# Attention bias from its 32 hidden units: relu tiles in float32 and one float32 product per tile, in place of on/off masks and two rounds of split bf16 products

## The chip, the cores and the metric

One core of a Trainium2 chip runs the whole program. The metric is the device time of one execution in microseconds (us); the kernel before takes 932.72 us (median of three runs, 932.68 to 932.83). The core's engines work side by side: PE (TensorE, matrix products; PEld is its weight load), DVE (VectorE), ACT (ScalarE), POOL (GpSimd), and SP (SyncE), which here only starts DMA transfers. Each engine runs its own instructions in the order in which they are written; semaphores make it wait for others.

## The reference, cut to what matters

Attention with a learned position bias is followed by two dense blocks, which the change leaves alone. The bias is computed once and used by all four batches:

```python
pos = np.arange(S)                                    # S = 576
psi_rel = np.log1p(np.abs(rel))                       # rel = i - j
psi_i = np.log1p(np.maximum(pos[:, None], 1.0))
x = (psi_rel / psi_i)[..., None]
h = np.maximum(x @ w1 + b1, 0.0)                      # 32 hidden units
bias = h @ w2                                         # 8 heads
scores = scores + bias.transpose(2, 0, 1)[None]
```

For one row i, x depends on |i - j| alone. So a row of the bias is a table over the distance 0, 1, 2, ..., laid out once forwards and once mirrored. Everything is float32 at the interface.

## The kernel before, in words

The program has four stages one after another: the bias (class `Bias`), attention, a gated block and a last block. Only the first stage and what hands it over are touched.

`Bias` works in 36 groups of 16 rows i; `order` takes groups 32 to 35 first and then 0 to 31. Group g needs `width(g)` distances: 304 to 576, summed over the 36 groups 15840, so 440 on average. A group has 4 tiles. A tile has 128 partitions, which are 4 rows times 32 hidden units, and along it lie the distances; `self.lt` holds log1p of the distance in every partition. The weights of the second layer are set up so that the product of a tile gives 32 partitions (4 rows times 8 heads), which go to one quarter of the columns of PE's array (`tile_position=(0, 32 * q)`). The four tiles of a group so fill one PSUM tile `ps` of 128 partitions (16 rows times 8 heads).

Before, `masks` (L163) does not compute relu. It writes a bf16 tile `mk` that says where a unit is on (1 or 0): ACT does 7 of 16 tiles with a steep sigmoid (L169), DVE the others with a comparison (L171). What the unit then adds is a line in x, a slope and a constant, both linear in the mask. `products(n, 0)` multiplies the masks by the slopes, DVE multiplies the result in PSUM by x (L207), and `products(n, 1)` adds the constants, one group later, into the same PSUM tile. The weights `cb` are float32 numbers split into three bf16 parts, so each of the two rounds takes 3 products per tile, or 6 where the width is over 512 (`parts` is 2). All products are on L189.

Then ACT copies `ps` to `rs` (L214), POOL writes the mirrored half beside it (`pool_round`, L54; for the last group DVE, L218), SP writes `rs` to DRAM (`write`, on L47, 295.5 KB), and `beside(n)` puts one step of the first attention pair behind it on POOL's or SP's queue: loads of q, k, v, their split into high and low parts on POOL, moves of these by DMA, and `load_bias`, which reads finished rows of the bias back from DRAM. The numbers 24, 27 and 30 in `beside` say behind which group.

`AHEAD = 2`: the tiles of a group are made two groups before their products. There are 17 buffers for `mk`, 6 for `rs` and 4 PSUM tiles, which are all of PSUM. When the stage ends its pools are closed, and attention's take the same memory: the first scores wait for PSUM from the last copies, and the last two bias tiles are read back once the last write has landed.

Of the kernel before, what the change touches and what calls it, by code (L numbers as in the profile page):

```python
# [17 lines left out]
S = 576  # L18
# [65 lines left out]
class Bias:  # L84
# [9 lines left out]
    ROW = 2 * S  # L94
    MID = S - 1
    AHEAD = 2
    ON_ACT = 7

    def __init__(self, ch, i, dram):
        self.ch, self.nc, self.i = ch, ch.nc, i  # L100
# [24 lines left out]
    def open(self):  # L125
        ch, nc, i = self.ch, self.nc, self.i
        cp = ch.pool(self.ctx, "bc", "right")
        self.wp = ch.pool(self.ctx, "bw", "right")
        self.pp = ch.pool(self.ctx, "bp", "right", bufs=4, space=PSUM)
        con = cp.tile([128, 194], F, name="con")  # L130
        self.lt = cp.tile([128, S], F, name="lt")
        nc.sync.dma_start(con, i["small"])
        nc.scalar.dma_start(self.lt, i["ltab"])
        sm, ip4, self.ip16 = con[:, :14], con[:, 14:158], con[:, 158:194]
        self.nb = cp.tile([128, 2], F, name="nb")
        self.scl = cp.tile([128, 144], F, name="scl")
        self.scb = cp.tile([128, 144], F, name="scb")
        cab = cp.tile([128, 16], F, name="cab")
        cf = cp.tile([128, 2, 32], F, name="cf")
        self.cb = cp.tile([128, 3, 2, 32], B, name="cb")  # L140

        self.warm = cp.tile([128, 2], F, name="warm")
        nc.gpsimd.memset(self.warm, 0.0)
        nc.scalar.activation(self.warm, self.warm, AF.Sigmoid)
        ts = nc.vector.tensor_scalar
        big = float(2.0**60)
        ts(out=self.nb[:, 1:2], in0=sm[:, 1:2], scalar1=big, scalar2=None, op0=ALU.mult)
        ts(out=self.scb, in0=ip4, scalar1=sm[:, 0:1], scalar2=big, op0=ALU.mult, op1=ALU.mult)
        ts(out=self.nb[:, 0:1], in0=sm[:, 1:2], scalar1=-1.0, scalar2=None, op0=ALU.mult)
        ts(out=self.scl, in0=ip4, scalar1=sm[:, 0:1], scalar2=None, op0=ALU.mult)  # L150
        for ab in range(2):
            ts(out=cab[:, 8 * ab : 8 * ab + 8], in0=sm[:, 2:10], scalar1=sm[:, ab : ab + 1], scalar2=8.0, op0=ALU.mult, op1=ALU.mult)

            nc.vector.tensor_tensor(
                out=cf[:, ab].rearrange("p (r h) -> p r h", r=4), in0=sm[:, 10:14].unsqueeze(2).to_broadcast([128, 4, 8]),
                in1=cab[:, 8 * ab : 8 * ab + 8].unsqueeze(1).to_broadcast([128, 4, 8]), op=ALU.mult,
            )
        for n in range(3):
            nc.vector.tensor_copy(self.cb[:, n], cf)
            if n < 2:  # L160
                nc.vector.tensor_tensor(out=cf, in0=cf, in1=self.cb[:, n], op=ALU.subtract)

    def masks(self, g):  # L163
        out = []
        w = self.width(g)
        for t in range(4 * g, 4 * g + 4):
            m = self.wp.tile([128, S], B, tag="mk", name="mk", bufs=4 * self.AHEAD + 9)
            if (self.no * self.ON_ACT) % 16 < self.ON_ACT:
                self.nc.scalar.activation(m[:, :w], self.lt[:, :w], AF.Sigmoid, bias=self.nb[:, 1:2], scale=self.scb[:, t : t + 1])  # L169
            else:  # L170
                self.nc.vector.tensor_scalar(  # L171
                    out=m[:, :w], in0=self.lt[:, :w], scalar1=self.scl[:, t : t + 1], scalar2=self.nb[:, 0:1], op0=ALU.mult, op1=ALU.is_gt
                )
            self.no += 1
            out.append(m)
        return out

    def run(self, beside):
        nc = self.nc
        order = list(range(32, 36)) + list(range(32))  # L180
        mq = [self.masks(g) for g in order[: self.AHEAD]]
        G = {}

        def products(n, ab):
            ps, mk, parts, ln = G[n]
            for at in range(parts):
                for part in range(3):
                    for q in range(4):
                        nc.tensor.matmul(  # L189
                            ps[32 * q : 32 * q + 32, at, :ln], self.cb[:, part, ab], mk[q][:, at * ln : at * ln + ln],  # L190
                            start=ab == part == 0, stop=part == 2, tile_position=(0, 32 * q), skip_group_check=ab > 0,
                        )

        for n in range(len(order) + 1):
            if n < len(order):
                g = order[n]
                w = self.width(g)
                parts = 1 if w <= 512 else 2
                ps = self.pp.tile([128, 2, 512], F, tag="ps", name="ps")
                ln = w // parts  # L200
                G[n] = (ps, mq.pop(0), parts, ln)
                products(n, 0)
                if n + self.AHEAD < len(order):
                    mq.append(self.masks(order[n + self.AHEAD]))
                a = ps[:, :parts, :ln]
                lt = self.lt[:, :w].rearrange("p (a b) -> p a b", a=parts)
                nc.vector.scalar_tensor_tensor(out=a, in0=lt, scalar=self.ip16[:, g : g + 1], in1=a, op0=ALU.mult, op1=ALU.mult)  # L207
            if n:
                g = order[n - 1]
                w, r = self.width(g), 16 * g + 15  # L210
                products(n - 1, 1)
                ps, _, parts, ln = G.pop(n - 1)
                rs = self.wp.tile([128, 2 * S], F, tag="rs", name="rs", bufs=6)
                nc.scalar.copy(rs[:, r : r + w].rearrange("p (a b) -> p a b", a=parts), ps[:, :parts, :ln])  # L214
                if n < len(order):
                    self.ch.pool_round(rs[:, :r], rs[:, r + 1 : 2 * r + 1][:, ::-1])
                else:
                    nc.vector.tensor_copy(rs[:, :r], ps[:, 0, 1 : r + 1][:, ::-1])  # L218
                self.write(g, rs)
                beside(n - 1)  # L220
        nc.scalar.activation(self.warm, self.warm, AF.Exp)


class Attention:
# [320 lines left out]
class Gated:  # L545
# [11 lines left out]
    def __init__(self, ch, i, x_d, x2_d, gw_d, g_d):  # L557
# [669 lines left out]
def tile_kernel(tc, i, out):  # L1227
    with tc.manual_schedule(), tc.tile_pool(name="dram", bufs=1, space=DRAM) as dp:
        x_d = [dp.tile([2, DM, S], F, name="x_d%d" % b) for b in range(NB)]
        x2_d = [dp.tile([DM, TC], F, name="x2_d%d" % c) for c in range(NC)]  # L1230
        gw_d = dp.tile([FF, DM], F, name="gw_d")
        g_d = [dp.tile([FF, TC], F, name="g_d%d" % c) for c in range(NC)]
        ch = Chip(tc)

        ga = Gated(ch, i, x_d, x2_d, gw_d, g_d)
        ga.open_keep()
        bias = Bias(ch, i, dp)
        bias.open()
        at = Attention(ch, i, bias, x_d, ga)
        at.open_left()  # L1240

        def beside(n):

            at.start(n)
            if n == 7:
                at.load_bias(0, 0)
            if n in (1, 2):
                at.load_ab(n - 1)
            if n == 24:
                at.load_bias(0, 1, 2)  # L1250
            if n == 27:
                at.load_bias(0, 5, 6)
            if n == 30:
# [96 lines left out]
```

## Time and profile before

| | us |
|---|---|
| median of the runs | 932.72 |
| the profiled execution | 937.69 |
| its span | 935.9 |
| first and last on/off tile begun on DVE | 6.2 and 64.2 |
| last write of the stage issued | 70.0 |
| DVE busy between 6 and 70 | 61.5 of 64 |

The span runs from the first to the last instruction of the profiled execution; 1.8 us lie around it, and the profiled execution is 5.0 us longer than the median of the runs. A view by stretches gives each engine's busy time in a stretch; a timeline gives start, length and form of instructions, with neighbours of one kind merged (x7). A length there can run past the start of the next instruction on the same engine, so the cost of one is read from start to start.

### The profile page before, as it was taken

What the parts mean: (1) busy time and instruction counts of PE and PEld (TensorE: products, weight loads), DVE (VectorE), ACT (ScalarE), POOL (GpSimd) and SP (SyncE); (2) the same over time, 40 slices, a digit from 0 to 9 for tenths busy, and PEclk for the clock granted to TensorE, in tenths of its full rate; (3) what the DMA queues carried; (4) which work ended last, traced back from release to release, by engine and by line L of the source; (5) the groups of instructions that cost most, each with busy time, mean ns of one, the idle gap of its engine ahead of it and who ended that gap; (6) DMA issues with size and microseconds to landing.
All of it is one profiled execution on the core that took longest, in us unless ns stands there. A gap on an engine that the chain in (4) does not pass through costs nothing.

```text
span 935.9 us, 16914 instructions
## 1 busy us (share of the span) xinstructions
PE 862.0 (92%) x5836; PEld 780.1 (83%) x5836; DVE 665.2 (71%) x1497; ACT 509.6 (54%) x1081; POOL 394.7 (42%) x460
## 2 busy tenths in 40 slices
PE   5877999999989988988999998999999999999998
PEld 4446998998989977987889888999999788888886
DVE  8989998998979988887764286752445765555442
ACT  7986998998878954434332133241333644444432
POOL 3337888887868643020110003742234442222200
PEclk9998999999999999998999999999999999999999
DMA  4997999898898667674351385673323211111001
GB/s 135 302 308 201 219 275 248 228 270 233 205 272 219 159 208 231 204 240 155 133 166 34 124 271 173 229 225 99 112 87 111 82 34 55 48 46 46 23 23 46
DMA packets 98389, 151.60 MB, mean 162 GB/s; under 512 B 16384, under 2 KB 62848, under 8 KB 98304
## 3 DMA queue, kind: packets, MB, share of 16 engines
q1 hardware_dynamic: 91248, 140.80, 51.3%
q10 hardware_dynamic: 7056, 9.74, 2.9%
q8 instruction: 46, 0.75, 0.3%
q14 instruction: 39, 0.32, 0.1%
HBM read 81.40 MB, written 41.30 MB: 131 GB/s over the span
## 4 chain that ended last, share of the span: by engine, by line
PE 59%; DVE 19%; DMA 12%; issue 5%; ACT 3%; SPq 2%; POOL 1%; ACTq 0%; DVEq 0%; POOLq 0%
PE ab L79 5%; PE ab L80 5%; PE ab L81 5%; DMA k<-kr 4%; PE op L463 4%; PE tp L420 4%; PE o L80 4%; PE o L79 4%; PE o L81 4%; PE sp L379 4%; DVE mk L171 3%; PE x L80 3%; PE x L81 3%; PE x L79 3%; DVE etl L511 2%
## 5 line engine op out<-in xcount | busy, mean ns | idle before, releaser
L79 PE MATMUL ab<-xh,ab 128*128 128x384 f32 x320 | 109.8, 343 | 7.7 <-DVE a L795 5.4
L410 POOL TENSOR_SCALAR e<-e,st 128x576 f32<-128x576 f32 x128 | 95.0, 752 | 33.9 <-DVE st L406 28.2
L80 PE MATMUL ab<-xl,ab 128*128 128x384 f32 x320 | 108.7, 340 | 0.0
L81 PE MATMUL ab<-xh,ab 128*128 128x384 f32 x320 | 108.7, 340 | 0.0
L511 DVE TENSOR_TENSOR etl<-tp,eth 128x512 fp32r<-128x512 f32 (+1 forms) x160 | 99.3, 629 | 8.8 <-ACT eth L497 6.7
L379 PE MATMUL sp<-k,q 128*128 128x288 f32 x512 | 91.0, 302 | 15.2 <-DVE st L392 6.4
L399 ACT ACTIVATE e<-e,st 128x576 f32<-128x576 f32 x128 | 100.1, 782 | 5.7 <-DVE st L392 5.5
L392 DVE CUSTOM_DVE_ANT_0 e<-sp,bt 128x576 f32<-128x576 f32 x128 | 95.6, 748 | 8.5 <-PE sp L379 8.3
L497 ACT CAST eth<-tp 128x512 fp32r<-128x512 f32 (+1 forms) x160 | 85.2, 543 | 28.7 <-PE tp L420 22.2
L747 POOL TENSOR_TENSOR xs<-xh,xl 128x384 f32<-128x384 f32 x20 | 24.2, 1224 | 173.6 <-DMA xl<-x_d 47.6
L420 PE MATMUL tp<-idt,e 128*128 128x128 f32 x576 | 88.7, 277 | 8.5 <-DVE etl L511 4.5
L379 PEld LDWEIGHTS sp<-k,q 128*128 128x128 f32 x512 | 76.3, 192 | 17.8 <-issue 7.8
L420 PEld LDWEIGHTS tp<-idt,e 128*128 128x128 f32 x576 | 70.0, 142 | 13.5 <-issue 6.0
L80 PE MATMUL x<-gl,wf 128*128 128x384 f32 x192 | 65.9, 343 | 8.5 <-DVE gl L62 8.5
L79 PEld LDWEIGHTS ab<-xh,ab 128*128 128x128 f32 x320 | 60.9, 190 | 11.2 <-DVE a L795 7.8
L189 PE MATMUL ps<-mk,cb 128*32 128x264 bf16 (+17 forms) x1056 | 48.8, 323 | 19.8 <-DVE ps L207 12.5
L463 PE MATMUL op<-eth,v 128*128 128x288 f32 x256 | 66.3, 340 | 0.4 <-ACT o L499 0.4
L1175 POOL TENSOR_TENSOR st<-st,half 128x1 f32<-128x1 f32 x18 | 9.9, 552 | 131.9 <-DVE st L1174 131.9
L79 PE MATMUL x<-gh,wf 128*128 128x384 f32 x192 | 65.1, 339 | 0.0
L81 PE MATMUL x<-gh,wf 128*128 128x384 f32 x192 | 65.1, 339 | 0.0
L189 PEld LDWEIGHTS <-cb 128*32 128x32 bf16 x1056 | 31.2, 98 | 37.0 <-issue 24.0
L80 PEld LDWEIGHTS ab<-xl,ab 128*128 128x128 f32 x320 | 61.0, 190 | 0.4 <-DVE xl L756 0.4
(209 smaller groups left out, 2355.7 us busy)
## 6 DMA issues: line engine op xcount, KB each, us to landing
bias_d<-rs SPq DMA_DIRECT2D x36, 295.5 KB, 4.5
qkr<-in_qk SPq DMA_DIRECT2D x16, 608.0 KB, 5.4
k<-kr SPq DMA_DIRECT2D x32, 288.0 KB, 6.5
x_d<-o SPq DMA_DIRECT2D x64, 144.0 KB, 3.9
g_d<-a ACTq DMA_DIRECT2D x48, 192.0 KB, 2.9
gl<-g_d SPq DMA_DIRECT2D x48, 192.0 KB, 2.8
k<-kr SPq DMA_DIRECT2D x32, 256.0 KB, 6.4
raw<-in_wo SPq DMA_DIRECT2D x16, 512.0 KB, 5.6
```

The source lines that it names most:

```text
L79: mm(out, a[0], b[0], start=first, stop=False, skip_group_check=more)
L80: mm(out, a[0], b[1], start=False, stop=False, skip_group_check=more)
L81: mm(out, a[1], b[0], start=False, stop=last, skip_group_check=more)
L189: nc.tensor.matmul(ps[32 * q : 32 * q + 32, at, :ln], self.cb[:, part, ab], mk[q][:, at * ln : at * ln + ln], start=ab == part == 0, stop= ...
L379: nc.tensor.matmul(ps[:, half, :HS], w["q"][:, h, q * 128 : q * 128 + 128], w["k"][:, h, x, half * HS : half * HS + HS], start=x == 0, sto ...
L392: self.nc.vector.tensor_tensor_reduce(out=halves(e), in0=ps[:, :, :HS], in1=halves(self.BT[(self.pairs[n][0], k)]), scale=-0.125, scalar=3e38,
L399: self.nc.scalar.activation(e, e, AF.Exp, bias=st[:, c : c + 1], scale=-1.0, accum_out=st[:, 2 + c : 3 + c])
L410: self.nc.gpsimd.tensor_scalar(out=e, in0=e, scalar1=st[:, c : c + 1], scalar2=1.0, op0=ALU.mult, op1=ALU.mult)
L420: tr = lambda c, src: nc.tensor.transpose(ps[: src.shape[1], c * 128 : c * 128 + 128], src, self.idt)
L463: nc.tensor.matmul(w["op"][:, half, :HS], lhs, rhs, start=c == 0 and x == 0, stop=c == 4 and x == 1)
L497: self.nc.scalar.copy(hi, src)
L511: self.nc.vector.tensor_tensor(out=lo, in0=src, in1=hi.bitcast(F), op=ALU.subtract)
```

## The change: what it does, and the diff

`masks` now makes relu itself, in float32, in a whole group at a time: groups with n % 8 in (2, 6), 9 of 36, on ACT (Relu), the other 27 on DVE, which takes the larger of scale times distance and minus b1, that is relu less a constant. One float32 product per tile (two where the width is over 512) takes the place of the 6 or 12 bf16 ones. DVE's work in PSUM (L207) is gone. ACT's copy adds the constant that DVE's groups lack: `cst`, which PE makes once at the start from the biases. There are 14 buffers for `mk`, each of twice the bytes; the read-backs in `beside` come one group earlier, the last group is mirrored on POOL, and the table of ACT's functions that is loaded at the start is already the one that attention uses.

```diff
-            m = self.wp.tile([128, S], B, tag="mk", name="mk", bufs=4 * self.AHEAD + 9)
-            if (self.no * self.ON_ACT) % 16 < self.ON_ACT:
-                self.nc.scalar.activation(m[:, :w], self.lt[:, :w], AF.Sigmoid, bias=self.nb[:, 1:2], scale=self.scb[:, t : t + 1])
+            m = self.wp.tile([128, S], F, tag="mk", name="mk", bufs=4 * self.AHEAD + 6)
+            if self.on_act(n):
+                self.nc.scalar.activation(m[:, :w], self.lt[:, :w], AF.Relu, bias=self.nb[:, 1:2], scale=self.scl[:, t : t + 1])
             else:
                 self.nc.vector.tensor_scalar(
-                    out=m[:, :w], in0=self.lt[:, :w], scalar1=self.scl[:, t : t + 1], scalar2=self.nb[:, 0:1], op0=ALU.mult, op1=ALU.is_gt
+                    out=m[:, :w], in0=self.lt[:, :w], scalar1=self.scl[:, t : t + 1], scalar2=self.nb[:, 0:1], op0=ALU.mult, op1=ALU.max
                 )
...
+    def on_act(self, n):
+        return n % 8 in (2, 6)
...
+        ps = self.pp.tile([128, 2, 512], F, tag="ps", name="ps")
+        for q in range(4):
+            nc.tensor.matmul(ps[32 * q : 32 * q + 32, 0, :2], self.cf, self.nb, start=True, stop=True, tile_position=(0, 32 * q))
+        nc.vector.tensor_copy(self.cst[:, 0:1], ps[:, 0, 1:2])
...
             for at in range(parts):
-                for part in range(3):
-                    for q in range(4):
-                        nc.tensor.matmul(
-                            ps[32 * q : 32 * q + 32, at, :ln], self.cb[:, part, ab], mk[q][:, at * ln : at * ln + ln],
-                            start=ab == part == 0, stop=part == 2, tile_position=(0, 32 * q), skip_group_check=ab > 0,
-                        )
...
-                nc.vector.scalar_tensor_tensor(out=a, in0=lt, scalar=self.ip16[:, g : g + 1], in1=a, op0=ALU.mult, op1=ALU.mult)
...
-                nc.scalar.copy(rs[:, r : r + w].rearrange("p (a b) -> p a b", a=parts), ps[:, :parts, :ln])
-                if n < len(order):
-                    self.ch.pool_round(rs[:, :r], rs[:, r + 1 : 2 * r + 1][:, ::-1])
-                else:
-                    nc.vector.tensor_copy(rs[:, :r], ps[:, 0, 1 : r + 1][:, ::-1])
...
+                for q in range(4):
+                    nc.tensor.matmul(
+                        ps[32 * q : 32 * q + 32, at, :ln], self.cf, mk[q][:, at * ln : at * ln + ln],
+                        start=True, stop=True, tile_position=(0, 32 * q),
+                    )
+            if n + self.AHEAD < len(order):
+                mq.append(self.masks(n + self.AHEAD, order[n + self.AHEAD]))
+            rs = self.wp.tile([128, 2 * S], F, tag="rs", name="rs", bufs=6)
+            c = 1 if self.on_act(n) else 0
+            nc.scalar.activation(
+                rs[:, r : r + w].rearrange("p (a b) -> p a b", a=parts), ps[:, :parts, :ln], AF.Identity, bias=self.cst[:, c : c + 1], scale=1.0
+            )
+            self.ch.pool_round(rs[:, :r], rs[:, r + 1 : 2 * r + 1][:, ::-1])
```

On DVE, from the end of the setup on, this stood in a row before (`mk` are the on/off tiles, the row with `ps` is the work in PSUM):

```order
L159 CAST cb<-cf 128x64
L171 TENSOR_SCALAR mk<-lt,scl,nb 128x528 x2
L171 TENSOR_SCALAR mk<-lt,scl,nb 128x544 x2
L171 TENSOR_SCALAR mk<-lt,scl,nb 128x560 x3
L207 SCALAR_TENSOR_TENSOR ps<-lt,con,ps 128x2x264
L171 TENSOR_SCALAR mk<-lt,scl,nb 128x576 x2
L207 SCALAR_TENSOR_TENSOR ps<-lt,con,ps 128x2x272
```

The same place of the changed kernel, where `mk` are relu tiles and `cst` is the constant that PE has just made:

```order
L149 TENSOR_TENSOR cf<-con,w_98 128x32
L177 COPY cst<-ps 128x1
L162 TENSOR_SCALAR mk<-lt,scl,nb 128x528 x4
L162 TENSOR_SCALAR mk<-lt,scl,nb 128x544 x4
L162 TENSOR_SCALAR mk<-lt,scl,nb 128x576 x8
L162 TENSOR_SCALAR mk<-lt,scl,nb 128x560 x4
L162 TENSOR_SCALAR mk<-lt,scl,nb 128x528 x4
```

The work in PSUM is out of the row, whole groups follow each other, and one copy that waits for PE stands ahead of the first tile.

On ACT the stage began so before (`rs` is the copy out of PSUM):

```order
L169 ACTIVATE mk<-lt,nb,scb 128x528 x2
L169 ACTIVATE mk<-lt,nb,scb 128x544 x2
L169 ACTIVATE mk<-lt,nb,scb 128x560
L169 ACTIVATE mk<-lt,nb,scb 128x576 x2
L214 COPY rs<-ps 128x528
L169 ACTIVATE mk<-lt,nb,scb 128x576 x2
L214 COPY rs<-ps 128x544
```

And so it begins in the changed kernel:

```order
L160 ACTIVATE mk<-lt,nb,scl 128x560 x4
L195 ACTIVATE rs<-ps,cst 128x528
L195 ACTIVATE rs<-ps,cst 128x544
L195 ACTIVATE rs<-ps,cst 128x560
L195 ACTIVATE rs<-ps,cst 128x576
L160 ACTIVATE mk<-lt,nb,scl 128x544 x4
L195 ACTIVATE rs<-ps,cst 128x576
```

ACT's tiles and copies, which took turns, now come in blocks of four and four.

## Rows read from the trace of the kernel before

**Rows 1.** The page's busy tenths, 40 slices of 23.4 us, DVE and DMA.

```profile
DVE  8989998998979988887764286752445765555442
DMA  4997999898898667674351385673323211111001
```

**Rows 2.** Busy us (instructions) by stretch, first column the stretch.

```profile
6.00:70.00 64.00, 49.40 (x1061) 31.88 (x1060) 61.50 (x121) 56.40 (x98) 24.63 (x40) 1.00 0.81 265
13.50:70.00 56.50, 43.23 (x922) 27.06 (x917) 54.03 (x106) 50.79 (x90) 23.66 (x39) 1.00 0.91 300
...
40.00:50.00 10.00, 7.80 (x188) 5.20 (x180) 10.00 (x24) 10.00 (x23) 3.67 (x8) 1.00 0.97 328
```

**Rows 3.** Timeline of DVE: start us, length us, what.

```profile
6.18 3.40 DVE L171 TENSOR_SCALAR mk<-lt,scl,nb 128x528 bf16<-128x528 f32 x7
9.51 0.76 DVE L207 SCALAR_TENSOR_TENSOR ps<-lt,con,ps 128x528 f32<-128x528 f32 x1
10.18 1.06 DVE L171 TENSOR_SCALAR mk<-lt,scl,nb 128x576 bf16<-128x576 f32 x2
11.16 0.78 DVE L207 SCALAR_TENSOR_TENSOR ps<-lt,con,ps 128x544 f32<-128x544 f32 x1
...
42.07 0.77 DVE L171 TENSOR_SCALAR mk<-lt,scl,nb 128x304 bf16<-128x304 f32 x2
42.76 0.56 DVE L207 SCALAR_TENSOR_TENSOR ps<-lt,con,ps 128x336 f32<-128x336 f32 x1
43.24 1.12 DVE L171 TENSOR_SCALAR mk<-lt,scl,nb 128x304 bf16<-128x304 f32 x3
...
74.21 0.74 DVE L70 TENSOR_SCALAR wab<-wab 128x512 f32<-128x512 f32 x2
```

**Rows 4.** Timeline of POOL and DVE, five rows where both work.

```profile
19.28 1.72 POOL L57 TENSOR_TENSOR ql<-qkr,qh 128x640 fp32r<-128x640 f32 x1
20.22 1.88 DVE L171 TENSOR_SCALAR mk<-lt,scl,nb 128x512 bf16<-128x512 f32 x2
22.02 0.77 DVE L207 SCALAR_TENSOR_TENSOR ps<-lt,con,ps 128x544 f32<-128x544 f32 x1
22.59 0.22 POOL L54 TENSOR_SCALAR rs<-rs 128x15 f32<-128x15 f32 x1
...
41.10 0.38 POOL L54 TENSOR_SCALAR rs<-rs 128x207 f32<-128x207 f32 x1 [1.00 <-ACT rs L214]
```

**Rows 5.** Timeline of PE: the first product, a full group, attention's products and transposes.

```profile
5.35 0.40 PE L189 MATMUL ps<-mk,cb 128*32 128x264 bf16 x1 [5.35 <-DVE cb L159]
...
16.02 1.64 PE L189 MATMUL ps<-mk,cb 128*32 128x288 bf16 x48 [0.39 <-DVE ps L207]
...
101.35 0.29 PE L79 MATMUL sp<-kr,qh 128*128 128x288 f32 x1
101.48 0.30 PE L80 MATMUL sp<-kr,qh 128*128 128x288 f32 x1
...
102.14 0.60 PE L420 MATMUL tp<-idt,e 128*128 128x128 f32 x4
102.50 0.51 PE L463 MATMUL op<-elh,v 128*128 128x288 f32 x2
```

**Rows 6.** Timeline of ACT, two on/off tiles and a copy.

```profile
40.89 1.23 ACT L169 ACTIVATE mk<-lt,nb,scb 128x320 bf16<-128x320 f32 x2
42.00 0.48 ACT L214 COPY rs<-ps 128x368 f32<-128x368 f32 x1
```

**Rows 7.** Timeline of all engines where the stage ends.

```profile
67.79 0.83 PE L189 MATMUL ps<-mk,cb 128*32 128x512 bf16 x12 [0.30 <-DVE ps L207]
...
68.71 0.59 ACT L214 COPY rs<-ps 128x512 f32<-128x512 f32 x1 [0.56 <-PE ps L189]
...
69.33 0.69 DVE L218 COPY rs<-ps 128x511 f32<-128x511 f32 x1 [1.59 <-ACT rs L214]
...
73.17 1.27 SPq L47 DMA_DIRECT2D bt<-bias_d  x3
```

More of the change, by code (lines that the diff above doesn't have):

```diff
@@ L96 @@
     AHEAD = 2
-    ON_ACT = 7
+    ON_ACT = 11
     def __init__(self, ch, i, dram):
@@ L136, in open, with masks @@
         self.scl = cp.tile([128, 144], F, name="scl")
[L137 to L140, printed above, removed]
+        self.w8 = cp.tile([128, 8], F, name="w8")
+        self.cf = cp.tile([128, 32], F, name="cf")
+        self.cst = cp.tile([128, 2], F, name="cst")
+        nc.gpsimd.memset(self.cst, 0.0)
         self.warm = cp.tile([128, 2], F, name="warm")
         nc.gpsimd.memset(self.warm, 0.0)
-        nc.scalar.activation(self.warm, self.warm, AF.Sigmoid)
+        nc.scalar.activation(self.warm, self.warm, AF.Exp)
         ts = nc.vector.tensor_scalar
-        big = float(2.0**60)
-        ts(out=self.nb[:, 1:2], in0=sm[:, 1:2], scalar1=big, scalar2=None, op0=ALU.mult)
-        ts(out=self.scb, in0=ip4, scalar1=sm[:, 0:1], scalar2=big, op0=ALU.mult, op1=ALU.mult)
+        ts(out=self.scl, in0=ip4, scalar1=sm[:, 0:1], scalar2=None, op0=ALU.mult)
         ts(out=self.nb[:, 0:1], in0=sm[:, 1:2], scalar1=-1.0, scalar2=None, op0=ALU.mult)
[L150 to L156, printed above, removed]
-            )
[L158 to L163, printed above, removed]
+        ts(out=self.nb[:, 1:2], in0=sm[:, 1:2], scalar1=1.0, scalar2=None, op0=ALU.mult)
+        ts(out=self.w8, in0=sm[:, 2:10], scalar1=8.0, scalar2=None, op0=ALU.mult)
+        nc.vector.tensor_tensor(
+            out=self.cf.rearrange("p (r h) -> p r h", r=4), in0=sm[:, 10:14].unsqueeze(2).to_broadcast([128, 4, 8]),
+            in1=self.w8.unsqueeze(1).to_broadcast([128, 4, 8]), op=ALU.mult,
+        )
+    def masks(self, n, g):
         out = []
@@ L194, in run @@
-        for n in range(len(order) + 1):
-            if n < len(order):
[L196 to L206, printed above, removed]
-                nc.vector.scalar_tensor_tensor(out=a, in0=lt, scalar=self.ip16[:, g : g + 1], in1=a, op0=ALU.mult, op1=ALU.mult)
[L208 to L213, printed above, removed]
-                nc.scalar.copy(rs[:, r : r + w].rearrange("p (a b) -> p a b", a=parts), ps[:, :parts, :ln])
-                if n < len(order):
-                    self.ch.pool_round(rs[:, :r], rs[:, r + 1 : 2 * r + 1][:, ::-1])
-                else:
-                    nc.vector.tensor_copy(rs[:, :r], ps[:, 0, 1 : r + 1][:, ::-1])
-                self.write(g, rs)
-                beside(n - 1)
@@ L221, in run @@
-        nc.scalar.activation(self.warm, self.warm, AF.Exp)
+        ps = self.pp.tile([128, 2, 512], F, tag="ps", name="ps")
+        for q in range(4):
+            nc.tensor.matmul(ps[32 * q : 32 * q + 32, 0, :2], self.cf, self.nb, start=True, stop=True, tile_position=(0, 32 * q))
+        nc.vector.tensor_copy(self.cst[:, 0:1], ps[:, 0, 1:2])
+        mq = [self.masks(n, g) for n, g in enumerate(order[: self.AHEAD])]
+        for n, g in enumerate(order):
+            w, r = self.width(g), 16 * g + 15
+            parts = 1 if w <= 512 else 2
+            ln = w // parts
+            mk = mq.pop(0)
+            ps = self.pp.tile([128, 2, 512], F, tag="ps", name="ps")
+            for at in range(parts):
+                for q in range(4):
[9 more added lines that the diff above has]
+                rs[:, r : r + w].rearrange("p (a b) -> p a b", a=parts), ps[:, :parts, :ln], AF.Identity, bias=self.cst[:, c : c + 1], scale=1.0
+            )
+            self.ch.pool_round(rs[:, :r], rs[:, r + 1 : 2 * r + 1][:, ::-1])
+            self.write(g, rs)
+            beside(n)
@@ L1248, in beside @@
                 at.load_ab(n - 1)
-            if n == 24:
+            if n == 23:
                 at.load_bias(0, 1, 2)
-            if n == 27:
+            if n == 26:
                 at.load_bias(0, 5, 6)
-            if n == 30:
+            if n == 29:
                 at.load_bias(0, 3)
```

6 lines of the change are left out of this document (removed).

## The prediction

> **What bounds the kernel now.** I first looked at the busy tenths of the page for the slices up to 70 us: DVE is at 8 to 9 there and DMA at 9 from the second slice on [rows 1]. The stretches say it in numbers: from 6 to 70 us DVE is busy 61.5 of 64 us, ACT 56.4, PE 49.4, POOL 24.6; from 13.5 us on, when writes flow, the DMA engines are 0.91 busy, and in the ten microseconds where writes dominate 0.97 [rows 2]. So DVE sets the pace of the bias stage, and DMA is close behind it. PE and ACT wait for DVE's work in PSUM. The end of the stage is a chain: the last 12 products, ACT's copy, the mirrored half, the last write, then the read-back at 73.17 [rows 7]. Attention's first scores hang on that copy and its last bias tiles on that write, so what the stage saves moves all that follows, as long as DMA keeps up.
>
> **DVE's part, which I take for the new bound.** Cost is read from start to start. Three on/off tiles: two of width 304 take 42.76 - 42.07 = 0.69, so 0.345 each; two of 576 take 0.98, so 0.49; seven of 528 to 560 take 3.33, so 0.476 [rows 3]. That is a line, 0.183 + 0.533 per 1000 distances, and at the mean width of 440 it gives 0.418 us. The work in PSUM costs 0.48 at 336 (42.76 to 43.24) and 0.67 at 528 (9.51 to 10.18) [rows 3], at 440 about 0.58, and 36 of them 20.9 us. DVE's 61.5 us less 20.9 and less 0.7 for the last copy [rows 7] leave 39.9 for its 81 on/off tiles, 0.493 each: 0.075 more than the line, 6.1 us in all. That excess is lost where POOL works: at 20.22 two tiles of 512 take 1.80 to the next start, the line says 0.91, and POOL is in a long subtraction from 19.28 to 21.00 [rows 4].
>
> Now DVE makes 27 x 4 = 108 tiles; their groups' widths sum to 11888, 440 on average. 108 x 0.418 = 45.1 us, if a float32 result costs what a bf16 one does. No bias row shows that, but the row at 74.21 does for another line: two float32 tiles of 512 from float32 in 0.74 together [rows 3], not above the line's 0.46 each. The lower end is then 0.37 at 512, a fifth off (36 us); the upper end is the price of the work in PSUM, 0.58, or 62.6 us. I take 45.1, because the row at 74.21 is the same kind of operation. The loss against POOL grows: before, tiles were 39.9 of DVE's 61.5 us, 65%, and POOL could work beside the rest for nothing; now DVE does nothing but tiles, so 6.1 / 0.65 = 9.4 us. Its ends are 6.1, as before, and 24.6, all of POOL's busy time [rows 2]. Together 54.5 us.
>
> A rule of the Trainium skill speaks against this change here ("SBUF — State Buffer", section "SBUF: two separate sides"): DVE in a two-port mode and POOL share one pair of ports as a lock, and whoever has it blocks the other for the whole instruction. By that rule all 24.6 us would be lost and the sum below would be 939.8; by the rows, where 6.1 of 0.65 x 24.6 = 16 us were lost, it is 926.7. The piece at 20.22 agrees with the rule, the stage as a whole shows 38% of it.
>
> **Start.** Before, the first tile on DVE starts at 6.18, behind the splitting of the weights [rows 3]. Seven small instructions of that go and one copy comes, which waits for a tiny product; the first product of before took 0.40 [rows 5]. The weights are ready some 0.6 us sooner and the copy with its wait costs about as much as was left, so I take 5.5 (between 5.2 and 6.2). Queued behind that waiting copy are all of DVE's tiles; ACT's first four don't wait for it.
>
> **PE.** The bf16 quarters run side by side: 48 products of 288 take 1.64 us, 34 ns each [rows 5], where one product of 288 over the whole array takes 130 ns (101.35 to 101.48). The new products read 63360 columns in all (4 tiles of 15840). No row shows a float32 product that isn't rounded to the short form. Lower end: as cheap as the rounded one and side by side, 63360 x 0.130 / 288 / 4 = 7.2 us. Upper end by the nearest row, the float32 transposes one after another: four of 128 columns in 0.36 us (102.14 to 102.50), 0.70 ns a column, 44.6 us. I take the upper end, since the transposes are PE's only unrounded float32 here; it lies under DVE's 54.5 and costs nothing. In the widest groups both come to nearly the same: 4 x 576 columns are 1.6 us, three quarters of a group's four tiles on DVE 1.5 plus the loss. Without DVE, PE alone would end the stage only some 10 us earlier.
>
> **ACT and POOL.** Two tiles of 320 on ACT take 1.11, a copy of 368 less than 0.48 [rows 6]. 36 tiles of 0.62 and 36 copies of 0.45 are 39 us: covered by DVE. But ACT's tiles come in blocks of four, some 2.5 us, and the copies of the next group wait behind them. What covers this is that 4 PSUM tiles let PE go on for that long (four groups are 6 us of DVE), and that a block starts two groups ahead of its use. POOL gets one more mirrored half and loses nothing. The read-backs keep their place in SP's queue but for one row.
>
> **The end.** From the last tile: one product still to come, 0.45 with its wait, copy 0.63, mirrored half 0.66, issue 0.1: 1.9 us, against 2.2 before from 67.79 to 70.02, where the mirrored half ends [rows 7].
>
> **Sum.** 5.5 + 54.5 + 1.9 = 61.9 for the last write, against 70.0: 8.1 us. DMA gives part back. It needs 0.91 x 56.5 = 51.4 us of full work from 13.5 to 70 [rows 2]; at 0.97 that is 53.0, so only 3.5 us can be squeezed out of it, and the rest of the gain must come from starting it earlier: the first group's four tiles now end at about 7.4 on DVE, its write can go at about 9.5 instead of 13, but for a few microseconds DMA then has little to carry. I take 2 us off (ends: 0, and 4.6, where only the 3.5 remain). 6 us of gain in the profiled execution, 937.69 - 6 = 931.7; the median of the runs stands 5.0 below that execution, so 926.7.
>
> **The rivals.** *PE becomes the bound, slower.* If an unrounded product goes four times over its columns and the quarters don't run side by side, each pass costs 0.130 / 288 us a column: 63360 x 0.451 ns = 28.6 us, four of them 114 us. The stage ends at 6 + 114 + 1.5 = 122, 52 us late: 985. For it: nothing here shows float32 quarters side by side. Against it: bf16 quarters are, and the four passes side by side would be 28.6 in all. It decides from 0.86 ns a column on, where PE needs DVE's 54.5. At half the clock the 44.6 us would be 89, a stage end at 97 and 955; the granted clock is 1.00 through the stage [rows 2]. The four passes are what the Trainium skill states for true float32 ("FP8 and Floating Point Precision", "TensorE Precision Notes"); no row here can show them.
>
> *DVE and POOL take turns, slower.* With all of POOL's 24.6 us lost, DVE needs 69.7, the write goes at 77.1, 7.1 late: 939.8. With a float32 result at the price of the work in PSUM it would be 942. It decides from a loss of 15.5 us on, where the 6 us are used up.
>
> *DMA holds the end.* The same bytes go out, the engines are at 0.91 already, and a backlog at the end delays the read-back that attention waits for: gain 0 to 3 us, 930 to 934, about 932.
>
> *More than forecast.* DVE as cheap as the row at 74.21, DMA in no one's way: 8 to 12 us, 920 to 923.
>
> **How the numbers follow.** The forecast has 0.50, with its own range 923 to 930. PE as the bound 0.18, DVE and POOL in turns 0.10, DMA 0.14, more than forecast 0.08. What a measurement tells from no change is 0.2%, 1.9 us: faster below 930.9, same up to 934.6. DMA's case lies mostly within that, a little of it below: faster 0.50 + 0.08 + 0.02 = 0.60, same 0.12, slower 0.28. The range leaves out PE as the bound (0.18) and the far end of the gain: 921 to 943.
>
> **What would show it.** Right: tiles on DVE from start to start near 0.5, DVE busy to the end of the stage, ending near 60, the last write near 62, PE's products in `ps` under 45 us. Wrong: DVE idle for products or buffers (PE is the bound), tiles above 0.6 (POOL), SP or ACT waiting for writes to land (DMA). If the stage ends near 62 and the time has not moved, the loss lies in attention's first pair.

## The result, and the profile after

The changed kernel takes 945.15 us (median of four runs, 940.86 to 947.54) beside 932.78 us of the kernel before on the same chip: a ratio of 1.0124, 95% interval 1.008 to 1.0168. It is slower by 8 to 16 us where 6 us of gain was forecast. The profiled execution took 943.03 us, its span is 941.2.

The page, with the rows of busy tenths that answer to [rows 1] (slices of 23.5 us), POOL's row and the granted clock:

```profile
span 941.2 us, 15450 instructions
...
DVE  8477998998989977988664276842445775555542
...
POOL 5436888787887763012010023742335442222200
PEclk9788999999999989998999999999999999999999
DMA  0898889899899667665451376663424211111001
```

DVE falls to 4 in the second slice, and DMA, which carried 4 tenths in the first slice of before, carries nothing there now. The stretches show where (columns: length, then busy us and instructions of PE, PEld, DVE, ACT and POOL, the granted clock, DMA share, GB/s):

```profile
10.00:20.00 10.00, 9.91 (x116) 4.34 (x108) 10.00 (x23) 6.34 (x9) 10.00 (x1) 1.00 0.01 2
20.00:30.00 10.00, 1.44 (x7) 0.25 (x4) 4.61 (x11) 0.71 (x1) 5.75 (x2) 0.73 0.38 106
30.00:40.00 10.00, 6.22 (x32) 2.38 (x32) 2.76 (x6) 5.32 (x8) 7.42 (x13) 0.59 0.97 335
...
60.00:70.00 10.00, 8.29 (x58) 3.22 (x62) 9.51 (x21) 9.24 (x18) 4.21 (x8) 1.00 1.00 332
```

From 10 to 20 us DMA moves almost nothing (0.01), and POOL is "busy" for all 10 us with a single instruction. From 20 us on PE, DVE and ACT stand still, and the clock that PE is granted falls to 0.73 and 0.59, after PE had nothing to do; later DMA runs full to make up for it. The timeline of the same time (start, length, what, in brackets the idle time before and what ended it):

```profile
5.21 19.41 DVE L162 TENSOR_SCALAR mk<-lt,scl,nb 128x528 f32<-128x528 f32 x42
10.00 15.75 POOL L54 TENSOR_SCALAR rs<-rs 128x527 f32<-128x527 f32 x2 [9.15 <-ACT rs L195]
11.12 0.71 ACT L195 ACTIVATE rs<-ps,cst 128x544 f32<-128x544 f32 x1 [1.22 <-PE ps L187]
12.06 0.73 ACT L195 ACTIVATE rs<-ps,cst 128x560 f32<-128x560 f32 x1 [0.23 <-PE ps L187]
13.04 0.74 ACT L195 ACTIVATE rs<-ps,cst 128x576 f32<-128x576 f32 x1 [0.24 <-PE ps L187]
...
16.60 1.34 ACT L195 ACTIVATE rs<-ps,cst 128x576 f32<-128x576 f32 x2
...
25.15 0.32 SPq L47 DMA_DIRECT2D bias_d<-rs  x1
...
27.62 0.71 ACT L195 ACTIVATE rs<-ps,cst 128x544 f32<-128x544 f32 x1 [9.68 <-DMA bias_d<-rs]
33.78 6.46 PE L187 MATMUL ps<-mk,cf 128*32 128x480 f32 x32 [12.34 <-ACT mk L160]
35.63 1.23 DVE L162 TENSOR_SCALAR mk<-lt,scl,nb 128x432 f32<-128x432 f32 x2 [11.02 <-PE ps L187]
...
54.67 10.14 DVE L162 TENSOR_SCALAR mk<-lt,scl,nb 128x320 f32<-128x320 f32 x24 [1.25 <-PE ps L187]
55.91 0.42 POOL L54 TENSOR_SCALAR rs<-rs 128x255 f32<-128x255 f32 x1 [0.53 <-ACT rs L195]
...
83.49 1.27 SPq L47 DMA_DIRECT2D bt<-bias_d  x3
```

Read it from the top. DVE makes 42 tiles without a pause, 0.462 us each; the prediction's line for their mean width (519) says 0.460, so DVE loses nothing to POOL. POOL's first two mirrored halves take 15.75 us together where before one took under 1 us. The tile `rs`, all 36 mirrored halves (shortest, median and longest in ns):

```profile
L54 POOL TENSOR_SCALAR rs<-rs x36: 222/516/15123, 10.0 to 76.9; 128x527 f32<-128x527 f32 x1, 128x543 f32<-128x543 f32 x1, 128x559 f32<-128x559 f32 x1, 128x575 f32<-128x575 f32 x1
L47 SPq DMA_DIRECT2D bias_d<-rs x36: 319/420/1746, 25.1 to 78.4; - x36
```

The very first half is the one of 15.1 us. It gets in when DVE stops. So the first write goes at 25.15, against 12.9 before, and the last at 78.4, against 70.0. The waits say how the rest of the machine came to a halt (us in total, times, longest):

```profile
PEld ps L187 <- ACT mk L160: 34.9, 29, 13.2
...
ACT rs L195 <- DMA bias_d<-rs: 22.0, 9, 9.7
...
DVE mk L162 <- PE ps L187: 19.5, 6, 11.0
```

No write leaves, so the 6 `rs` buffers fill (the sixth copy is done at 17.9); ACT's next copy waits for a write to land (9.68 before 27.62); ACT's four tiles of a later group stand behind that copy in its row; PE waits for those tiles (12.34 before 33.78); PE frees no tile buffers, and DVE waits for one (11.02 before 35.63). It is this last wait that finally lets POOL in. Only the first row of tiles keeps POOL out like this: from 54.67 on DVE makes 24 tiles without a stop, and POOL's halves get in between them (0.42 us at 55.91). What sets the first row apart is not shown. The read-back, at 73.17 before [rows 7], comes at 83.49.

### The profile page after: what moved, and what is told of

Read it like the earlier page. It is cut to its first block, busy times and chain, and to the rows that moved or that the text cites. A ratio compares the mean times of both kernels' runs of the same rounds, so it can differ in the third digit from the quotient of the medians.

```text
span 941.2 us, 15450 instructions
## 1 busy us (share of the span) xinstructions
PE 863.0 (92%) x5140; PEld 768.7 (82%) x5140; DVE 647.7 (69%) x1480; ACT 495.1 (53%) x1052; POOL 410.0 (44%) x462
## 4 chain that ended last, share of the span: by engine, by line
PE 64%; DVE 14%; DMA 11%; issue 4%; ACT 3%; POOL 3%; SPq 1%; ACTq 0%; DVEq 0%; POOLq 0%
PE ab L79 5%; PE ab L80 5%; PE ab L81 5%; PE op L442 5%; PE tp L399 5%; PE sp L358 5%; PE o L80 4%; PE o L79 4%; PE o L81 4%; PE x L80 3%; PE x L81 3%; PE x L79 3%; DVE etl L490 2%; PE ps L187 2%; DVE e L371 2%
## 5 line engine op out<-in xcount | busy, mean ns | idle before, releaser
L79 PE MATMUL ab<-xh,ab 128*128 128x384 f32 x320 | 108.4, 339 | 5.0 <-DVE a L774 2.2
L81 PE MATMUL ab<-xh,ab 128*128 128x384 f32 x320 | 107.5, 336 | 0.0
L726 POOL TENSOR_TENSOR xs<-xh,xl 128x384 f32<-128x384 f32 x20 | 27.4, 1379 | 165.9 <-DMA xl<-x_d 139.1
L80 PE MATMUL x<-gl,wf 128*128 128x384 f32 x192 | 65.1, 339 | 7.6 <-DVE gl L62 7.6
L187 PE MATMUL ps<-mk,cf 128*32 128x272 f32 (+17 forms) x352 | 49.8, 538 | 21.2 <-ACT mk L160 19.7
L442 PE MATMUL op<-eth,v 128*128 128x288 f32 x256 | 66.5, 341 | 0.4 <-ACT o L478 0.4
L162 DVE TENSOR_SCALAR mk<-lt,scl,nb 128x528 f32<-128x528 f32 (+17 forms) x108 | 48.8, 525 | 19.9 <-PE ps L187 19.5
L187 PEld LDWEIGHTS ps<-mk,cf 128*32 128x32 f32 x352 | 18.6, 121 | 51.6 <-ACT mk L160 34.9
```

The source lines that it names most:

```text
L79: mm(out, a[0], b[0], start=first, stop=False, skip_group_check=more)
L80: mm(out, a[0], b[1], start=False, stop=False, skip_group_check=more)
L81: mm(out, a[1], b[0], start=False, stop=last, skip_group_check=more)
L187: nc.tensor.matmul(ps[32 * q : 32 * q + 32, at, :ln], self.cf, mk[q][:, at * ln : at * ln + ln], start=True, stop=True, tile_position=(0, ...
L442: nc.tensor.matmul(w["op"][:, half, :HS], lhs, rhs, start=c == 0 and x == 0, stop=c == 4 and x == 1)
```

## The experiments

Theory 1: POOL is starved. A row of DVE tiles without anything between them keeps POOL out until DVE stops. Theory 2: ACT's tiles, now in blocks of four ahead of copies, make the chain of waits. A third view: the tile buffers decide. All edits are against the changed kernel unless another is named; the runs of before on the same chip are the measure.

**e1_gap.** One small reduction on DVE behind each of its 27 groups of four tiles, whose result nobody uses.

```diff
+        self.junk = cp.tile([128, 288], F, name="junk")
...
+        if not self.on_act(n):
+            self.nc.vector.tensor_reduce(out=self.junk[:, :1], in_=self.lt[:, :128], axis=AX.X, op=ALU.max)
```

> The changed kernel with 27 instructions more on DVE: behind each of its groups of four tiles a maximum over 128 elements, which reads one tensor of SBUF and writes one column. Theory 1 (starved): DVE's tiles, run without a pause, keep POOL from starting; in the changed kernel its first mirrored half took 15.1 us and the first write went at 25.1. A pause of some 0.25 us in which DVE does something else lets POOL in: the first mirrored half ends by 11 us, the first write goes by 12, no mirrored half takes over 4 us, and 7 us more work on DVE make the kernel faster, 925 to 935. Theory 2 (blocks): the stalls come from ACT's four tiles in a row, behind which copies and products wait; then the added work changes nothing or costs up to 7 us, 943 to 955. Theory 3 (too few tile buffers): as theory 2.

Measured: 930.21 us (925.49 to 934.12, 10 runs), ratio to before 0.9952 (0.9927 to 0.9977). Its timeline:

```profile
7.10 0.28 DVE L168 TENSOR_REDUCE junk<-lt 128x1 f32<-128x128 f32 x1
...
9.38 2.36 DVE L163 TENSOR_SCALAR mk<-lt,scl,nb 128x576 f32<-128x576 f32 x4
10.03 0.91 POOL L54 TENSOR_SCALAR rs<-rs 128x527 f32<-128x527 f32 x1 [9.18 <-ACT rs L198]
...
16.47 4.35 DVE L163 TENSOR_SCALAR mk<-lt,scl,nb 128x528 f32<-128x528 f32 x4
17.99 1.70 POOL L57 TENSOR_TENSOR ql<-qkr,qh 128x640 fp32r<-128x640 f32 x1
...
61.21 1.27 SPq L47 DMA_DIRECT2D bt<-bias_d  x3
62.58 4.22 SPq L47 DMA_DIRECT2D bias_d<-rs  x6
...
71.37 1.27 SPq L47 DMA_DIRECT2D bt<-bias_d  x3
```

The first mirrored half takes 0.91 us, the write follows at 11, and ACT waits 3.1 us for landings in place of 22.0. Now DVE pays: four tiles of 528 take 4.35 us beside POOL's splits, where 1.9 is their price. An added instruction of 0.2 us, 27 times, makes the kernel some 16 us faster (1.0124 - 0.9952, times 932.8), to below before.

**e2_control.** The same place, but a short tile: the operation of the relu tiles over 128 distances.

```diff
+            self.nc.vector.tensor_scalar(
+                out=self.junk[:, :128], in0=self.lt[:, :128], scalar1=self.scl[:, 0:1], scalar2=self.nb[:, 0:1], op0=ALU.mult, op1=ALU.max
+            )
```

> As the run before, but the instruction that is added 27 times is one more short tile of the same kind as DVE's others (128 elements, scaled and compared, some 0.25 us), not a maximum. It costs DVE the same time. Theory 1: such an instruction keeps POOL out as the tiles do, so the first mirrored half takes 12 us or more again and the time stays at 940 to 955. If only DVE's slower pace helped in the run before, this run is as fast as that one.

Measured: 943.19 us (941.05 to 944.66, 7 runs), ratio 1.0084 (1.0056 to 1.0112). The time is that of theory 1; the picture is not quite:

```profile
9.98 4.82 POOL L54 TENSOR_SCALAR rs<-rs 128x527 f32<-128x527 f32 x2 [9.13 <-ACT rs L200]
18.84 0.82 DVE L168 TENSOR_SCALAR junk<-lt,scl,nb 128x128 f32<-128x128 f32 x1
19.55 2.54 POOL L54 TENSOR_SCALAR rs<-rs 128x559 f32<-128x559 f32 x1
22.05 3.37 POOL L57 TENSOR_TENSOR ql<-qkr,qh 128x640 fp32r<-128x640 f32 x1
```

The 12 us for which POOL was expected to be shut out did not come: up to 30 us it gets one operation through per group, at the short tile, which then takes 0.82 where 0.34 is usual. With two operations and more per group to do it still falls behind: ACT waits 21.1 us for landings, the last write goes at 78.5. So it isn't DVE's pace that e1_gap changed, but what kind of instruction stands in its row.

**e3_bufs8.** 8 buffers for the tiles in place of 14, so that DVE can't run ahead.

```diff
-            m = self.wp.tile([128, S], F, tag="mk", name="mk", bufs=4 * self.AHEAD + 6)
+            m = self.wp.tile([128, S], F, tag="mk", name="mk", bufs=4 * self.AHEAD)
```

> The changed kernel with 8 buffers for the tiles in place of 14. Theory 1: DVE runs out of buffers sooner and pauses, so POOL gets in earlier: the first mirrored half takes under 5 us, the first write goes before 16 us, and fewer buffers make the kernel faster, 928 to 940. Theory 3: DVE's 19.5 us of waiting for buffers grow, and the time with them, 950 or more. Theory 2: near 945.

Measured: 936.22 us (930.67 to 940.13, 10 runs), ratio 1.0029 (0.9996 to 1.0061).

```profile
10.19 6.59 DVE L162 TENSOR_SCALAR mk<-lt,scl,nb 128x576 f32<-128x576 f32 x12 [1.23 <-PE ps L187]
12.03 1.53 POOL L54 TENSOR_SCALAR rs<-rs 128x527 f32<-128x527 f32 x2 [11.18 <-ACT rs L195]
17.54 12.85 DVE L162 TENSOR_SCALAR mk<-lt,scl,nb 128x528 f32<-128x528 f32 x20 [0.77 <-PE ps L187]
```

Fewer buffers make it faster, which a lack of tile buffers as the cause can't explain. DVE has to wait for PE early (1.23 us before 10.19), and afterwards two mirrored halves take 1.53 us beside its tiles. The first half gets in at once, 1.8 us after the row of 12 tiles began and with nothing else between them. So an unbroken row alone doesn't keep POOL out. That DVE's earlier wait opened the way is likely, but not shown.

**e4_tilewise.** ACT makes one tile of every group in place of all four of every fourth; its constant goes to the three other quarters alone.

```diff
-            if self.on_act(n):
+            if t % 4 == 3:
...
-        nc.vector.tensor_copy(self.cst[:, 0:1], ps[:, 0, 1:2])
+        nc.vector.tensor_copy(self.cst[0:96, 0:1], ps[0:96, 0, 1:2])
...
-            c = 1 if self.on_act(n) else 0
+            c = 0
```

> The changed kernel with ACT making the last tile of every group in place of all four of every fourth group; DVE makes three of each group, 108 in all as before, and the constant is left out for that quarter. Theory 2: without blocks of four the stalls go, under 932. Theory 1: DVE still runs without a pause until its buffers are used up behind a blocked ACT, some 14 us; the first mirrored half takes 8 us or more, the first write goes after 17 us, 934 to 945.

Measured: 943.24 us (935.12 to 950.96, 10 runs), ratio 1.0097 (1.0063 to 1.0132).

```profile
5.25 18.54 DVE L162 TENSOR_SCALAR mk<-lt,scl,nb 128x528 f32<-128x528 f32 x40
9.62 15.31 POOL L54 TENSOR_SCALAR rs<-rs 128x527 f32<-128x527 f32 x2 [8.77 <-ACT rs L195]
```

Without ACT's blocks the same thing happens: 40 tiles, POOL 14.7 us in its first half, 25.2 us of ACT's waits for landings. Theory 2 falls.

**e5_late.** e1_gap, with the read-backs moved behind groups 24, 28 and 33, to see whether SP's wait for landed rows (4.4 us in e1_gap) holds the writes behind it.

```diff
-            if n == 23:
+            if n == 24:
...
-            if n == 26:
+            if n == 28:
...
-            if n == 29:
+            if n == 33:
```

> The run with the 27 pauses, and the read-backs of finished rows put behind groups 24, 28 and 33 in place of 23, 26 and 29. With the pauses the last write went at 66.5 us, 3.5 earlier than before, but landed only 1.8 earlier, and SP stood 4.4 us in front of the third read-back, with six writes queued behind it. If that wait is what the gain is lost to, the last write goes by 64, the read-back behind the stage comes at 69 or earlier in place of 71.4, and the time is 925 to 929. If DMA's own rate holds the end, the read-back stays at 71 and the time at 930.

Measured: 929.61 us (924.79 to 932.74, 12 runs), ratio 0.9972 (0.9955 to 0.9988). SP's wait (3.7 us) has only moved; the last write begins at 66.3 (65.8 in e1_gap, where the expectation has 66.5), the last read-back at 70.60, later than expected. The order on SP isn't what holds the rest; the outcome is near the other case, DMA's own rate, which no run tests by itself.

**e6_gap2.** e1_gap with two pauses per group, behind the second and the fourth tile.

```diff
+            if t % 2 and not self.on_act(n):
+                self.nc.vector.tensor_reduce(out=self.junk[:, :1], in_=self.lt[:, :128], axis=AX.X, op=ALU.max)
```

> The run with pauses, with two per group (54 in all), behind its second and fourth tile. Theory 1 in its plain form (a pause is all that POOL needs): mirrored halves start sooner, none takes over 2 us, but DVE has 5 us more work, so the end of its tiles goes from 62.3 to 65 or later and the time is 930 to 935. If one pause per group still starves POOL by much, it is faster, 924 to 929.

Measured: 932.11 us (923.88 to 938.64, 10 runs), ratio 0.9994 (0.9966 to 1.0023). The first mirrored half takes 0.98 us, no less than with one pause; the tiles end at 66.5 in place of 62.2. One pause per group is enough for the first half, and a second costs DVE 4.3 us; the intervals of the two times overlap.

**e7_copies.** No added instruction: DVE makes all 36 copies out of PSUM, which stand between its groups, and ACT the tiles of every second group in exchange.

```diff
-        return n % 8 in (2, 6)
+        return n % 2 == 0
...
-            nc.scalar.activation(
-                rs[:, r : r + w].rearrange("p (a b) -> p a b", a=parts), ps[:, :parts, :ln], AF.Identity, bias=self.cst[:, c : c + 1], scale=1.0
+            nc.vector.tensor_scalar(
+                out=rs[:, r : r + w].rearrange("p (a b) -> p a b", a=parts), in0=ps[:, :parts, :ln],
+                scalar1=self.cst[:, c : c + 1], scalar2=None, op0=ALU.add,
             )
```

> The changed kernel with the work shared out in another way, and no added instruction: DVE copies every group out of PSUM (it adds the constant there) and makes the tiles of every other group; ACT only makes tiles, those of the other 18 groups. DVE then reads PSUM once per group, as it did in the kernel before. Theory 1: this is a pause like the maximum, but does needed work; the first mirrored half takes under 2 us, the first write goes by 12 us, and the time is 924 to 931. Theory 2 (what stalls is ACT's order): as fast too, since ACT no longer copies, but a mirrored half can then still take 5 us or more. If DVE's order is to blame in general, DVE waiting for products before its copies, it is slower than 935.

Measured: 931.47 us (926.61 to 935.94, 12 runs), ratio 1.0 (0.9976 to 1.0024). POOL isn't starved (first half 0.90 us, first write 10.9, last write 66.7), but the time is that of before, just above the 924 to 931 expected: a useful instruction between the groups opens the way just as well, and this arrangement brings no gain over the wasted one.

**e8_pe2.** e1_gap with every product made twice.

```diff
-                for q in range(4):
+                for q in (0, 1, 2, 3, 0, 1, 2, 3):
```

> The run with pauses, with every product made twice (the second writes the same values over the first). In the changed kernel four float32 products of 576 columns took some 0.96 us where groups followed each other closely, 0.42 ns a column, or 26 us for all. Doubled that is 53 us, still under DVE's 57: the time stays within 4 us of 930. By the price that the prediction took from the transposes, 0.70 ns a column, it would be 89 us, the stage would end 25 us later and the time would be 955 or more.

Measured: 934.01 us (928.77 to 938.05, 10 runs), ratio 1.0027 (1.0 to 1.0053). The stretch of the stage, columns as above:

```profile
6.00:70.00 64.00, 63.09 (x704) 31.58 (x702) 56.77 (x134) 41.90 (x69) 24.04 (x39) 1.00 0.80 262
```

PE is now busy throughout and ends the stage: the last write begins at 71.5, 5.7 us behind that of e1_gap. Twice the prediction's 44.6 us would be 89 us; all products, twice, fit into some 64 us (the first begins at 5.7, the last at 69.4). That is 0.50 ns a column and not the 0.42 expected, so PE did not stay under DVE's 57 us; by the ratios the time is 7.0 us above e1_gap's, where at most 4 were expected.

**e9_odd.** e2_control's short tile in another form: 129 distances read in one piece and written as 3 pieces of 43.

```diff
-                out=self.junk[:, :128], in0=self.lt[:, :128], scalar1=self.scl[:, 0:1], scalar2=self.nb[:, 0:1], op0=ALU.mult, op1=ALU.max
+                out=self.junk[:, :132].rearrange("p (a b) -> p a b", a=3)[:, :, :43], in0=self.lt[:, :129], scalar1=self.scl[:, 0:1], scalar2=self.nb[:, 0:1], op0=ALU.mult, op1=ALU.max
```

> The short tile of e2_control again, the same operation on the same kind of operands, but 129 distances read in one piece and written as 3 pieces of 43, so that source and result can't be halved alike and VectorE can't take the two-port form for it. Theory 1 in the form that the form of the instruction decides: the short tile is slower from start to start than the 0.26 us in e2_control (0.3 to 0.4), and POOL gets in as in e1_gap: first mirrored half under 2 us, first write about 11, last write begun before 68, time 925 to 935. Rival: it is the reduction, or DVE's change from one operation to another, that opens the way: then POOL's first operations take over 2 us each as in e2_control, ACT waits some 20 us for writes to land, and the time is 940 to 946.

Measured: 932.56 us (928.88 to 936.37, 12 runs), ratio 0.9994 (0.9975 to 1.0014).

```profile
6.92 0.41 DVE L168 TENSOR_SCALAR junk<-lt,scl,nb 128x129 f32<-128x129 f32 x1
7.23 1.98 DVE L163 TENSOR_SCALAR mk<-lt,scl,nb 128x544 f32<-128x544 f32 x4
9.86 2.95 POOL L54 TENSOR_SCALAR rs<-rs 128x527 f32<-128x527 f32 x2 [9.01 <-ACT rs L200]
...
17.10 2.00 POOL L54 TENSOR_SCALAR qh<-qkr 128x640 fp32r<-128x640 f32 x1 [4.29 <-DMA qkr<-in_qk]
19.06 0.83 POOL L54 TENSOR_SCALAR rs<-rs 128x559 f32<-128x559 f32 x1
19.87 1.70 POOL L57 TENSOR_TENSOR ql<-qkr,qh 128x640 fp32r<-128x640 f32 x1
...
42.06 13.70 POOL L54 TENSOR_SCALAR rs<-rs 128x207 f32<-128x207 f32 x11 [2.39 <-ACT rs L200]
```

The short tile takes 0.31 us from start to start, against 0.26 in e2_control, and from 19.06 to some 32 us POOL gets in between the tiles; the half of 559 and the subtraction, 2.54 and 3.37 us in e2_control, take 0.83 and 1.70. The same operation at the same place, slower by itself, takes 8.4 us off the time (1.0084 - 0.9994, times 932.8). So the form of the instruction counts, as theory 1 had it. (This tile is also 0.05 us longer, which was not told apart; e10_short speaks against length.) But the form doesn't open the way throughout: eleven halves from 42.06 on take 13.70 us, six of them 1.58 to 1.95 each, and most of these get in only at the short tile of the next group; in e1_gap none takes over 0.91. Three numbers missed: the longest half is 2.13 us (under 2 expected), the first write at 12.0, the last at 69.3. The first half, too, got in only at the short tile of 11.39, while in e1_gap it got in between two tiles. A reduction opens the way wider than this form does.

**e10_short.** e1_gap with the reduction over 8 distances.

```diff
-            self.nc.vector.tensor_reduce(out=self.junk[:, :1], in_=self.lt[:, :128], axis=AX.X, op=ALU.max)
+            self.nc.vector.tensor_reduce(out=self.junk[:, :1], in_=self.lt[:, :8], axis=AX.X, op=ALU.max)
```

> e1_gap with the reduction over 8 distances in place of 128. Theory 1: what lets POOL in is the kind of instruction, not how long it lasts: first mirrored half about 0.9 us, each pause some 0.1 us shorter (27 of them: 2 to 3 us of DVE), last tile on DVE ends between 59.5 and 61.5, time 926 to 931. Rival: POOL needs a gap of some length to get in: first mirrored half over 2 us, ACT waits more than 10 us for writes to land, time above 935.

Measured: 926.73 us (920.03 to 931.27, 12 runs), ratio 0.9932 (0.9908 to 0.9956).

```profile
7.02 0.15 DVE L168 TENSOR_REDUCE junk<-lt 128x1 f32<-128x8 f32 x1
7.09 1.97 DVE L163 TENSOR_SCALAR mk<-lt,scl,nb 128x544 f32<-128x544 f32 x4
...
9.95 0.66 POOL L54 TENSOR_SCALAR rs<-rs 128x527 f32<-128x527 f32 x1 [9.10 <-ACT rs L198]
```

And of its waits:

```profile
DVE mk L163 <- PE ps L190: 3.1, 3, 1.3
```

0.07 us of DVE is enough. The tiles end at 62.2, not at 59.5 to 61.5: DVE waits 3.1 us for products, which it did not in e1_gap, and that is as much as the pauses save. PE's granted clock from 6 to 70 us was 0.95 here and 1.00 there. This version beats both kernels; against e1_gap, on another chip, its interval overlaps.

**All together.** What each kernel's last write is late by, against 70.0 before, beside what its time differs by (ratio less 1, times 932.8 us):

| kernel | last write begins | late by | time differs by |
|---|---|---|---|
| changed | 78.4 | +8.4 | +11.6 |
| e4_tilewise | 78.9 | +8.9 | +9.0 |
| e2_control | 78.5 | +8.5 | +7.8 |
| e8_pe2 | 71.5 | +1.5 | +2.5 |
| e9_odd | 69.3 | -0.7 | -0.6 |
| e6_gap2 | 69.2 | -0.8 | -0.6 |
| e3_bufs8 | 68.0 | -2.0 | +2.7 |
| e10_short | 66.9 | -3.1 | -6.3 |
| e7_copies | 66.7 | -3.3 | 0.0 |
| e5_late | 66.3 | -3.7 | -2.6 |
| e1_gap | 65.8 | -4.2 | -4.5 |

The write column is of one execution, the time of many, with intervals of 1.5 to 4 us to either side. What the stage saves or loses moves the end by about as much, as the prediction took it. Three fall out: e3_bufs8 lies 1.6 us outside its interval (-0.4 to +5.7 us), e7_copies and e10_short 1 us outside theirs; why stays open.

## Why the prediction was wrong

**The step that failed** is in "ACT and POOL": "POOL gets one more mirrored half and loses nothing". I priced the contest of DVE and POOL from one side, as what DVE loses (9.4 us, with 6.1 and 24.6 as ends), and never as what POOL loses. In the changed kernel's first row the tiles run at the line's price and POOL stands for 15.1 us. e1_gap, e2_control and e9_odd show the cause, e4_tilewise takes the other one away. The rows of before had a hint in sight: 7 tiles follow each other on DVE at the start [rows 3], 2 or 3 later, and then comes the work in PSUM. I read that work as time in which POOL costs DVE nothing; I did not ask whether it also lets POOL in, as the copies out of PSUM do in e7_copies (0.90 us for the first half). My sign of failure, "tiles above 0.6 (POOL)", so looked on the wrong engine. The signs that did come, DVE idle for products (19.5 us) and ACT waiting for writes (22.0), I had put down to PE and to DMA.

**The rule that I weighed** was the right place. The Trainium skill ("SBUF — State Buffer", "SBUF: two separate sides") makes the shared pair of ports a lock whose loser fully blocks; I worked out the sum for DVE as the loser (939.8). The trace shows POOL as the loser for 15.1 us. By the Trainium skill, whichever starts first wins. Here POOL's half was ready at 10.00 and some 31 tiles were started ahead of it (14.6 us at 0.46), which that sentence doesn't say. The Trainium skill says further that `tensor_reduce` never contends ("SBUF — State Buffer", "Who interferes with whom"), and that the two-port mode wants source and destination with outermost dimensions both even or equal ("VectorE: DVE Perf Modes", "What auto-detection actually checks"). e9_odd, where they are 129 and 3, agrees with this by its 0.31 us against 0.26 and by POOL's 0.83 against 2.54, up to some 32 us.

**The rival** "DVE and POOL take turns, slower" had the sign and nearly the size (939.8 to 942), at 0.10, but by another way: not DVE 69.7 us long, but a stop of everything behind a full set of `rs` buffers. That the size fits is luck. Once the starvation is removed, DVE does pay: in e1_gap its tiles and pauses take 5.24 to 62.21, 57.0 us; less 26 pauses of 0.2 that is 51.8, so 6.7 us lost to POOL beside the 45.1 of the line (9.4 forecast).

**What "covers" an edit.** "What covers this is that 4 PSUM tiles let PE go on": true of ACT's blocks (e1_gap keeps them and does not stall, e4_tilewise drops them and does), but the cover behind the copies is the 6 `rs` buffers, and those ran out at 16.6 to 17.9 us with no write out.

**Right, by measure.** Start: 5.21 (5.5, ends 5.2 to 6.2). Price of a tile: 0.462 at 519, with a float32 result at no extra cost. What follows the stage moves with it. The 2 us that DMA was to give back show at the read-back alone: in e1_gap the last write begins 4.2 us earlier and the last read-back 1.8 (71.37 against 73.17), and the time is still 4.5 less.

**Off in size.** PE at 0.70 ns a column: ACT's copies of groups of 544, 560 and 576 follow 0.94 and 0.98 us after each other while PE works without a pause (11.12, 12.06, 13.04), so 0.94 / 560 = 1.68 ns per distance for four tiles, 0.42 ns a column, and 26.6 us for 63360. (The group of 544 itself came 1.92 after the first copy, 9.20 to 11.12, at a granted clock of 1.00 too; why is not shown.) The rival's case of four passes with the quarters side by side was 28.6. The Trainium skill's four passes for true float32 ("FP8 and Floating Point Precision", "TensorE Precision Notes") agree with it. e8_pe2 shows that one such round more costs 5.7 us of the stage. The end: 1.9 us forecast from the last tile to the last write, 3.6 in e1_gap (62.2 to 65.8). The mirrored half ends there at 65.1, 2.9 after the tile, and SP, which begins its last six writes only at 62.58, gets to the last one later still.

The prediction's sum for the last write then reads, for e1_gap: start 5.24, tiles 51.8, pauses 5.2, end 3.6, together 65.8, where 5.5, 54.5 and 1.9 made 61.9. With the starvation removed the change gives 4.5 us (2.1 to 6.8) in e1_gap and 6.3 (4.1 to 8.6) in e10_short, where 6 were forecast; part of that nearness is luck, since the terms miss in both directions.

**Slips in the working.** By the prediction's own way of counting, the half clock gives some 959 and not 955 (a stage end at 97 is 27 late), a gain of 8 to 12 us is 921 to 925 and not 920 to 923, and eight instructions leave the setup, not seven. None of them moves the forecast.

## What to carry to other kernels

Where DVE and POOL share work, cost the contest from both sides, and ask of an edit that takes "other" work off DVE's row whether it leaves a long run of one-source tiles between SBUF and SBUF: POOL may stand for as long as that run, as it did here for 15.1 us in the first row, though not in later ones. A small instruction of another kind in between (here a reduction over 8 elements, 0.07 us, once in four tiles) is a cheap remedy, and a chain that ends in a limited set of buffers turns a short starvation into a stop of all engines. When an added instruction that does nothing makes a kernel faster, try a twin of it in another form, to learn which property counts.

## What the runs showed of the hardware that was not expected

- Who loses depends on what stood in DVE's row before: POOL waited 15.1 us beside tiles alone, one operation got in per short tile of the same kind (e2_control up to 30 us, 2.2 to 3.4 us each), and DVE was the one that lost after a reduction (four tiles of 528 in 4.35 us). What exactly opens the way is not settled. A reduction that ended before POOL was ready (9.18 to 9.38 in e1_gap, POOL at 10.03) still lets POOL in between two later tiles, and so do rows of 12 and 24 tiles that began after a wait of DVE (e3_bufs8 at 12.03, the changed kernel at 55.91).
- A float32 product in quarters of the array costs 0.42 ns a column with the four side by side, at a granted clock of 1.00; over the whole stage of e8_pe2 it was 0.50.
- PE's granted clock was 1.00 while it worked without a pause, 0.73 in the stretch in which it came to a halt and 0.59 in the next (near 1.2 GHz, the lower of its two levels, for most of it), when it began again after 12.3 us. What that cost beside the waits was not told apart.
- Single executions differ by several us outside the stage: from the last read-back to the end of the span 862.7 us in the profiled execution of before (935.9 - 73.17), 857.7 in that of the change, 852.3 in e10_short (924.0 - 71.72), where the work is the same. Differences of a few us between two profiled executions say nothing here; medians of ten runs do.
